# Sigmoid attention and a gated two-layer network on one core: the first group's keys loaded and transposed by slots, and one value product moved

## The chip, the cores and the metric

The kernel runs on one core of a Trainium2 chip. A core has five engines that work side by side, each through its own list of instructions in order: TensorE (PE in the profile; PEld is its weight load), VectorE (DVE), ScalarE (ACT), GpSimd (POOL) and SyncE (SP). Engines wait for one another through semaphores. Data moves between the chip's memory and the core's SBUF by 16 DMA engines; transfers are asked for by an instruction on SP (queue q1, "hardware dynamic" in the profile) or on POOL (queue q0, "software dynamic", which here also casts float32 to float16 on the way). Matmuls write PSUM. The metric is the device time of one execution in microseconds (us), the median of three.

## The reference: what is computed

```
scores = q @ k^T / sqrt(64) - log(448)        # 8 batches, 12 heads, 448 tokens, head size 64
attn   = sigmoid(scores)                      # no softmax: each entry by itself
x      = (attn @ v), heads side by side       # 3584 tokens x 768
h      = x @ w_in                             # 768 x 2048
g      = h * sigmoid(beta * h)
out    = g @ w_out                            # 2048 x 768, float32
```

## The kernel before

**Groups, slots, visits.** Four heads make a group (three groups a batch, 24 in all), two heads a slot. A group's q and k lie in SBUF as a tile `raw` of 128 rows: 32 rows for each head, and each row holds 14 tokens of that head side by side. So slot 0 of a group is rows 0 to 63, slot 1 rows 64 to 127. DVE transposes 32x32 blocks of pairs of float16 (`transpose`, L186 to L205) into `qT` and `kT`, where the tokens lie along the row and the head size along the partitions, in two halves e = 0, 1 that are added up in PSUM. The 448 keys of a head are cut in three tiles of 128 (jt = 0, 1, 2) and a rest of 64 (jt = 3, `JF`).

A visit computes scores for a group and lets ACT take the sigmoid. In the first batch the queries are taken in two halves of 224 (`QH`), and there a `half_visit` does two key tiles of both slots for one half: with second = 0 the tiles 0 and 1, with second = 1 tile 2 and the rest. Its matmuls (`score`, L213) each use 32 rows of the PE array, so four of them, two heads of two slots, stand beside one another. `weigh` (L224) is ACT's sigmoid over the score tile. The score tiles are PSUM buffers, three at first and two later. `attend` (L281) multiplies attention by the values of a group and has DVE cast the result to `xT` (L290).

**The dense layers** are cut into units: `dense1` (one 128-column chunk of the first layer with its sigmoid on ACT, L307, and product on DVE, L310) and `dense2` or `strassen` pieces of the second layer, all through L166. A list of these units in a fixed order, `fill`, is drawn on between the visits; `fill_units(n)` takes the next n.

**The start, written out by hand.** The stretch that the change touches is under `manual_schedule`: the program's order is each engine's order.

- SP loads the first half of group 0's queries and all of its keys as float32 into a staging place in the tile `gt` (L519), then the small beta vector (L548).
- POOL clears a small tile `dummy` (L525), with which ACT loads its sigmoid table (L526).
- PE runs `idle_units`: matmuls on a tile of zeros (`still`, L535), 9 ahead of the first visit and 4 or 2 behind each of the next ones.
- DVE casts the staged queries (L539) and transposes them; ACT and DVE cast half of the keys each (L541, L542); DVE transposes the keys in two instructions (L199, L203).
- POOL asks for everything else, one request behind the other: group 1's and 2's first query halves and keys (L110), the values (L131, L138), the second query halves, eight pieces of w_in (L148); later, behind waits for free buffers, the next group's q and k, two pieces of w_out (L156), the next values, and so on.
- Six half visits with the idle units between them, then the products with the values and the second query halves. From `share_psum(ctx, 2, 4)` on, half visits, dense units and `attend` calls alternate as the code lists them, up to the loop over all other visits, which a budget of estimated costs paces.

POOL's requests take turns on eight completion semaphores, so a request also waits until the one eight before it has landed.

Of the kernel before, what the change touches and what calls it, by code (L numbers as in the profile page):

```python
# [8 lines left out]
FP32 = mybir.dt.float32  # L9
FP16 = mybir.dt.float16  # L10
# [3 lines left out]
def kernel(  # L14
# [17 lines left out]
    P = 128  # L32
# [73 lines left out]
    def load_one(g: int, r: int, c0: int = 0, c1: int = NB):  # L106
        b, t = divmod(g, QPB)
        if g not in raws:
            raws[g] = rawp.tile([P, 2, NB, D], FP16, tag="raw", name="raw")
        nc.gpsimd.dma_start(  # L110
            out=raws[g][:, r, c0:c1].rearrange("p c d -> p (c d)"),
            in_=(q, k)[r][b, HQ * t : HQ * (t + 1)].rearrange("h (p c) d -> (h p) (c d)", c=NB)[
                :, c0 * D : c1 * D
            ],
        )
# [70 lines left out]
    def transpose(g: int, r: int, c0: int = 0, c1: int = NB):  # L186
        raw = raws[g][:, r]
        if r == 0:
            if g not in qT:
                qT[g] = qTp.tile([P, NB * BLK, PAIR], FP16, tag="qT", name="qT")  # L190
            nc.vector.transpose(  # L191
                out=in_order(g // QPB, qT[g][:, c0 * BLK : c1 * BLK]),
                in_=raw[:, c0:c1].rearrange("p c d -> p (c d)").bitcast(FP32),
            )
            return
        kT[g] = kTp.tile([P, S, PAIR], FP16, tag="kT", name="kT")
        to = kT[g].rearrange("p k e -> p (k e)").bitcast(FP32)
        frm = raw.rearrange("p c d -> p (c d)").bitcast(FP32).rearrange("p (c f) -> p c f", c=NB)
        nc.vector.transpose(  # L199
            out=to[:, 0 : JF * P].rearrange("p (j i q) -> p i j q", j=JF, i=HQ),  # L200
            in_=frm[:, 0:NF].rearrange("p (i j) f -> p i j f", j=JF),
        )
        nc.vector.transpose(  # L203
            out=to[:, JF * P :], in_=frm[:, NF:].rearrange("p c f -> p (c f)")
        )  # L205

    def score_tile():
# [41 lines left out]
                at_tiles[s, jt, 0] = at  # L249


    def half_visit(g: int, c0: int, second: int):
        slots = (2 * g, 2 * g + 1)
        scos = [score_tile() for _ in slots]
        plan = [(s, jt, sco, jt * QH) for jt in (0, 1) for s, sco in zip(slots, scos)]
        widths = [S, S]
        if second:
            plan = [(s, 2, sco, 0) for s, sco in zip(slots, scos)]
            plan += [(s, JF, scos[0], QH) for s in slots]
            widths = [S, QH]  # L260
        for i in range(0, len(plan), 2):
            for e in range(PAIR):
                for s, jt, sco, u0 in plan[i : i + 2]:
                    for hh in range(2):
                        score(sco, u0, s, jt, hh, e, c0, QH)
        ats = {id(sco): weigh(sco, n) for sco, n in zip(scos, widths)}
        for s, jt, sco, u0 in plan:
            at_tiles[s, jt, c0] = ats[id(sco)][:, :, u0 : u0 + QH]

    def attend(g: int, c0: int, n: int, part=(0, 1)):  # L270
        b, t = divmod(g, QPB)
        if b not in xTs:
            xTs[b] = xTp.tile([P, NHC, S], FP16, tag="xT", name="xT")
        slots = [2 * g + x for x in part]
        avs = [bank("av_ps") for _ in slots]
        todo = [(s, av, jt) for s, av in zip(slots, avs) for jt in range(JF)]
        for s, av, jt in todo + [(s, av, JF) for s, av in zip(slots, avs)]:
            at = at_tiles.pop((s, jt, c0))
            base, nk = (last_base(s), KL) if jt == JF else (0, P)
            for hh in range(2):  # L280
                nc.tensor.matmul(  # L281
                    av[hh * D : (hh + 1) * D, 0:n],
                    vs[b][base : base + nk, 2 * (s % NPAIR) + hh, jt],
                    at[base : base + nk, hh, 0:n],
                    start=(jt == 0),
                    stop=(jt == JF),
                    tile_position=(base, hh * D),
                )
        for s, av in zip(slots, avs):
            nc.vector.tensor_copy(out=xTs[b][:, s % NPAIR, c0 : c0 + n], in_=av[:, 0:n])  # L290
# [210 lines left out]
    def fill_units(n: int):  # L501
        for _ in range(n):
            fill[at_fill[0]][2]()
            at_fill[0] += 1
# [4 lines left out]
    with tc.manual_schedule():  # L509
        raws[0] = rawp.tile([P, 2, NB, D], FP16, tag="raw", name="raw")  # L510
        wide = gt.rearrange("p a b -> p (a b)").bitcast(FP32)
        cut = NH * D
        early = [(0, 0, NH), (1, 0, NB)]
        staged = {}
        at = 0
        for r, c0, c1 in early:
            staged[r] = wide[:, at : at + (c1 - c0) * D]
            at += (c1 - c0) * D
            nc.sync.dma_start(  # L519
                out=staged[r],  # L520
                in_=(q, k)[r][0, 0:HQ].rearrange("h (p c) d -> (h p) (c d)", c=NB)[
                    :, c0 * D : c1 * D
                ],
            )
        nc.gpsimd.memset(dummy, 0.0)  # L525
        nc.scalar.activation(out=dummy, in_=dummy, func=AF.Sigmoid, bias=0.0, scale=1.0)  # L526

        still = const.tile([P, 512], FP16, name="still")
# [4 lines left out]
        def idle_units(n: int):  # L533
            for _ in range(n):
                nc.tensor.matmul(idle, still[:, 0:P], still, start=True, stop=True)  # L535

        idle_units(9)
        raw = raws[0].rearrange("p r c d -> p r (c d)")
        nc.vector.tensor_copy(out=raw[:, 0, 0:cut], in_=staged[0])  # L539
        transpose(0, 0, 0, NH)  # L540
        nc.scalar.copy(out=raw[:, 1, cut:], in_=staged[1][:, cut:])  # L541
        nc.vector.tensor_copy(out=raw[:, 1, 0:cut], in_=staged[1][:, 0:cut])  # L542
        transpose(0, 1)
        for g in range(1, QPB):
            load_one(g, 0, 0, NH)
            load_one(g, 1)
        load_v(0)
        nc.sync.dma_start(out=beta_in[0:NDC], in_=moe_beta.rearrange("(c p) -> c p", p=P))  # L548
        for g in range(QPB - 1):
            load_one(g, 0, NH, NB)  # L550
        for c in range(WCH):
            if c == WCH // 2:
                load_one(QPB - 1, 0, NH, NB)
            load_w_in(c)
        for g in range(1, QPB):
            transpose(g, 0, 0, NH)
            transpose(g, 1)

        for g in range(QPB):
            for second in range(2):  # L560
                half_visit(g, 0, second)
                if 2 * g + second < 2 * QPB - 1:
                    idle_units(4 if g < QPB - 1 else 2)
        double_v_last(0)
        transpose(0, 0, NH, NB)
        attend(0, 0, QH)
# [20 lines left out]
        share_psum(ctx, 2, 4)  # L587
        fill_units(4)
        half_visit(1, QH, 0)
        fill_units(3)  # L590
        half_visit(1, QH, 1)
        transpose(2, 0, NH, NB)
        attend(0, QH, QH)
        fill_units(1)
        half_visit(2, QH, 0)
        fill_units(4)
        half_visit(2, QH, 1)
        attend(1, QH, QH)
        fill_units(3)
        attend(2, QH, QH)  # L600
        fill_units(1)
        transpose(QPB, 0)
# [97 lines left out]
```

## Time and profile before

| what | us |
|---|---|
| median of three runs | 383.44 (382.74 to 384.87) |
| the profiled execution | 383.27 |
| its span, first to last instruction | 381.5 |
| PE busy | 375.9 (99% of the span) |
| DVE, ACT, POOL busy | 231.9, 229.2, 66.4 |
| first real matmul (L213) starts at | 5.77 |
| first sigmoid (L224) starts at | 6.50 |

PE counts as busy in the idle units too. In the profile, a row of the timeline is: start, length, engine, line, operation, output <- inputs, shapes, how many instructions are merged in the row, and in brackets how long the engine was idle before it and what ended that. A row of a window is: the stretch, its length, then for PE, PEld, DVE, ACT and POOL the busy time with the number of instructions, then PE's granted clock (1.00 is full), the mean busy share of the DMA engines (packets that overlap count twice, so it can be over 1) and GB/s. A row of the chain of waits is: start, length, who held the chain that ended last.

### The profile page before, as it was taken

Reading aid. Unit: us, or ns where it says so; the run is one execution under the profiler, and the core shown is the slowest. Engines: PE = TensorE matmul, PEld = TensorE weight load, DVE = VectorE, ACT = ScalarE, POOL = GpSimd, SP = SyncE. Lnnn points to the kernel's source line nnn. Section 1 sums busy time; section 2 is a strip of 40 time slices with the busy share of each in tenths; the row PEclk is TensorE's granted clock in tenths of the full one; section 3 lists DMA queues with packets and bytes.
Section 4 is the critical chain, followed back from the end, with each engine's and each line's share of the span. In section 5 each row is a group of like instructions: output and inputs, shape, how many; then the busy total and the mean of one; then the engine's idle time right before and its main releaser. Section 6 shows DMA issues by size and latency. Waiting matters only on the chain.

```text
span 381.5 us, 8227 instructions
## 1 busy us (share of the span) xinstructions
PE 375.9 (99%) x3415; PEld 199.0 (52%) x3415; DVE 231.9 (61%) x439; ACT 229.2 (60%) x330; POOL 66.4 (17%) x114
## 2 busy tenths in 40 slices
PE   8999999999999999999999999999999999999996
PEld 3477744444654445444554445544455444555563
DVE  4357366775765557465775657665676665755761
ACT  5987756687356776577355792477752787435100
POOL 7842433140110410040110410112100000000000
PEclk9999999999999999999999999999999999999999
DMA  9999999755363930672363850649203300030033
GB/s 169 187 197 205 192 204 210 164 71 54 50 132 84 121 51 2 131 98 24 50 132 72 115 69 2 133 87 117 50 0 84 85 1 2 2 83 0 2 83 125
DMA packets 42405, 34.71 MB, mean 91 GB/s; under 512 B 21872, under 2 KB 38656, under 8 KB 42368
## 3 DMA queue, kind: packets, MB, share of 16 engines
q0 software_dynamic: 36688, 22.47, 43.5%
q1 hardware_dynamic: 5680, 11.71, 11.6%
q8 instruction: 27, 0.44, 0.5%
q14 instruction: 10, 0.08, 0.1%
HBM read 45.62 MB, written 11.01 MB: 148 GB/s over the span
## 4 chain that ended last, share of the span: by engine, by line
PE 88%; DMA 9%; POOL 1%; issue 0%; DVE 0%; POOLq 0%
PE m_ps L166 70%; PE sco L213 10%; PE av_ps L281 8%; DMA w_out<-in_moe_w_out_dram 5%; DMA w_in<-in_moe_w_in_dram 3%; DMA raw<-in_k_dram 2%; POOL w_in L148 1%; POOL raw L110 1%; POOL w_out L156 0%; DVE osb L342 0%; POOL dummy L525 0%; POOLq L684 0%
## 5 line engine op out<-in xcount | busy, mean ns | idle before, releaser
L224 ACT ACTIVATE attnT<-sco 128x896 f16<-128x896 f32 (+1 forms) x171 | 145.3, 902 | 81.2 <-PE sco L213 80.6
L166 PE MATMUL m_ps<-xT,w_in 128*128 128x448 f16 (+2 forms) x1014 | 154.7, 336 | 0.1
L310 DVE TENSOR_TENSOR gt<-m_ps,sg 128x448 f16<-128x448 f32 (+1 forms) x144 | 81.4, 572 | 81.1 <-ACT sg L307 77.6
L166 PEld LDWEIGHTS <-w_in 128*128 128x128 f16 (+1 forms) x1014 | 82.6, 101 | 68.8 <-issue 15.0
L307 ACT ACTIVATE sg<-m_ps,beta_sb 128x448 f32<-128x448 f32 (+1 forms) x144 | 84.2, 597 | 36.5 <-PE m_ps L166 29.5
L166 PEld LDWEIGHTS <-sum 128*64 128x64 f16 (+1 forms) x664 | 48.0, 104 | 33.6 <-issue 7.9
L213 PE MATMUL sco<-qT,kT 32*128 32x448 f16 (+3 forms) x864 | 51.9, 340 | 0.7 <-DVE kT L199 0.6
L166 PE MATMUL m_ps<-w_T,sum 128*128 128x384 f16 (+1 forms) x360 | 51.6, 327 | 0.0
L110 POOL DMA_DIRECT2D raw<-in_q_dram x26 | 14.3, 552 | 184.1 <-DVE kT L203 176.9
L430 DVE TENSOR_TENSOR osb<-m_ps,osb 128x384 f32<-128x384 f32 x60 | 33.3, 555 | 18.7 <-PE m_ps L166 16.9
L166 PEld LDWEIGHTS <-gt 128*128 128x128 f16 (+1 forms) x414 | 31.4, 103 | 24.0 <-issue 6.5
L281 PE MATMUL av_ps<-attnT,v 128*64 128x448 f16 (+3 forms) x432 | 40.2, 338 | 0.0
L400 DVE TENSOR_TENSOR sum<-gt 128x1024 f16<-128x1024 f16 x60 | 39.2, 678 | 0.1
L290 DVE CAST xT<-av_ps 128x448 f16<-128x448 f32 (+1 forms) x54 | 28.5, 568 | 15.2 <-PE av_ps L281 14.1
L166 PE MATMUL m_ps<-w_T,gt 128*64 128x384 f16 (+1 forms) x268 | 34.3, 327 | 0.0
L166 PE MATMUL m_ps<-w_out,sum 128*64 128x384 f16 (+1 forms) x304 | 33.8, 327 | 0.0
L281 PEld LDWEIGHTS <-v 128*64 128x64 f16 (+1 forms) x432 | 20.6, 108 | 18.8 <-issue 9.4
L213 PEld LDWEIGHTS <-kT 32*128 32x128 f16 (+1 forms) x864 | 13.7, 96 | 28.6 <-issue 26.0
L166 PE MATMUL m_ps<-w_out,gt 128*128 128x384 f16 (+3 forms) x146 | 22.7, 327 | 0.1
L131 POOL DMA_DIRECT2D v<-in_v_dram x32 | 19.8, 631 | 9.6 <-DMA w_in<-in_moe_w_in_dram 5.2
L191 DVE STREAM_TRANSPOSE qT<-raw 128x448 f32<-128x448 f32 (+1 forms) x27 | 16.7, 617 | 0.1
L433 ACT COPY osb<-m_ps 128x384 f32<-128x384 f32 x12 | 5.8, 481 | 16.8 <-DMA out_dram<-osb 8.6
(25 smaller groups left out, 90.0 us busy)
## 6 DMA issues: line engine op xcount, KB each, us to landing
out_dram<-osb SPq DMA_DIRECT2D x98, 96.0 KB, 1.9
raw<-in_k_dram POOLq DMA_DIRECT2D x23, 224.0 KB, 4.9
raw<-in_q_dram POOLq DMA_DIRECT2D x21, 224.0 KB, 3.8
v<-in_v_dram POOLq DMA_DIRECT2D x32, 144.0 KB, 6.7
w_in<-in_moe_w_in_dram POOLq DMA_DIRECT2D x8, 384.0 KB, 11.2
w_out<-in_moe_w_out_dram POOLq DMA_DIRECT2D x4, 768.0 KB, 13.0
v<-in_v_dram POOLq DMA_DIRECT2D x16, 48.0 KB, 6.4
out_dram<-osb SPq DMA_DIRECT2D x2, 384.0 KB, 3.0
```

The costliest lines, as they stand in the source:

```text
L110: nc.gpsimd.dma_start(out=raws[g][:, r, c0:c1].rearrange("p c d -> p (c d)"), in_=(q, k)[r][b, HQ * t : HQ * (t + 1)].rearrange("h (p c) d ...
L131: nc.gpsimd.dma_start(out=vs[b][i * BLK : (i + 1) * BLK, :, 0:JF].rearrange("p h j d -> p h (j d)"), in_=rows[:, :, JF * i * D : JF * (i + ...
L166: nc.tensor.matmul(to[c : c + step], hidden[:, c : c + step], weights, **({} if step == P else {"tile_position": (0, c)}), **flags,)
L191: nc.vector.transpose(out=in_order(g // QPB, qT[g][:, c0 * BLK : c1 * BLK]), in_=raw[:, c0:c1].rearrange("p c d -> p (c d)").bitcast(FP32),)
L213: nc.tensor.matmul(sco[base : base + nk, hh, u0 : u0 + n], kT[g][lo : lo + BLK, jt * P : jt * P + nk, e], qT[g][lo : lo + BLK, c0 : c0 + n ...
L224: nc.scalar.activation(out=at[:, :, 0:n], in_=sco[:, :, 0:n], func=AF.Sigmoid, bias=NEG_LOG_S, scale=MSCALE,)
L281: nc.tensor.matmul(av[hh * D : (hh + 1) * D, 0:n], vs[b][base : base + nk, 2 * (s % NPAIR) + hh, jt], at[base : base + nk, hh, 0:n], start ...
L290: nc.vector.tensor_copy(out=xTs[b][:, s % NPAIR, c0 : c0 + n], in_=av[:, 0:n])
L307: nc.scalar.activation(out=sg[:, 0:n], in_=m1[:, 0:n], func=AF.Sigmoid, bias=0.0, scale=beta_sb[:, dc : dc + 1])
L310: nc.vector.tensor_tensor(out=gt[:, dc, off : off + n], in0=m1[:, 0:n], in1=sg[:, 0:n], op=ALU.mult)
L400: nc.vector.tensor_tensor(out=sums[t, i], in0=x, in1=y, op=op)
L430: nc.vector.tensor_tensor(out=out, in0=in0, in1=in1, op=op)
```

## The change

- Group 0's keys come in two transfers, 64 rows (one slot) each, behind the queries' half. In the staging tile the keys now lie ahead of the queries.
- The clearing of `dummy` moves from POOL to DVE.
- The idle units ahead of the first visit are 8 in place of 9; one stands between the two slots of the first half visit, and 2 in place of 4 behind it.
- `transpose_keys` transposes key tiles j0 to j1 of some rows. For group 0: slot 0's tiles 0 and 1 are cast by ACT and transposed; then slot 1's (one tile cast by ACT, one by DVE) and transposed; then tile 2 and the rest of both slots are cast by DVE and transposed.
- The first half visit does all its matmuls of slot 0, then one idle unit, then those of slot 1, each with its own score tile; two matmuls stand side by side in place of four.
- Groups 1 and 2: keys are asked for ahead of the queries, and the transposes go tiles 0 to 2, queries, rest.
- The second query half of group 2 is asked for behind the fifth piece of w_in in place of the fourth.
- `attend(0, QH, QH)` goes right behind the next half visit, `half_visit(1, QH, 0)`; the fill units around it are dealt out anew (4, 3, 3, 3, 2, 1, 4 in place of 4, 3, 1, 4, 3, 1, 4) and stay 20 in all.

```diff
--- before.py
+++ after.py
@@ -193,15 +193,23 @@
                 in_=raw[:, c0:c1].rearrange("p c d -> p (c d)").bitcast(FP32),
             )
             return
-        kT[g] = kTp.tile([P, S, PAIR], FP16, tag="kT", name="kT")
-        to = kT[g].rearrange("p k e -> p (k e)").bitcast(FP32)
-        frm = raw.rearrange("p c d -> p (c d)").bitcast(FP32).rearrange("p (c f) -> p c f", c=NB)
+        transpose_keys(g, 0, JF, slice(0, P))
+        transpose_keys(g, JF, JF + 1, slice(0, P))
+
+    def transpose_keys(g: int, j0: int, j1: int, rows):
+        if g not in kT:
+            kT[g] = kTp.tile([P, S, PAIR], FP16, tag="kT", name="kT")
+        to = kT[g][rows].rearrange("p k e -> p (k e)").bitcast(FP32)
+        frm = raws[g][rows, 1].rearrange("p c d -> p (c d)").bitcast(FP32)
+        frm = frm.rearrange("p (c f) -> p c f", c=NB)
+        if j0 == JF:
+            nc.vector.transpose(
+                out=to[:, JF * P :], in_=frm[:, NF:].rearrange("p c f -> p (c f)")
+            )
+            return
         nc.vector.transpose(
-            out=to[:, 0 : JF * P].rearrange("p (j i q) -> p i j q", j=JF, i=HQ),
-            in_=frm[:, 0:NF].rearrange("p (i j) f -> p i j f", j=JF),
-        )
-        nc.vector.transpose(
-            out=to[:, JF * P :], in_=frm[:, NF:].rearrange("p c f -> p (c f)")
+            out=to[:, j0 * P : j1 * P].rearrange("p (j i q) -> p i j q", i=HQ, q=BLK),
+            in_=frm[:, 0:NF].rearrange("p (i j) f -> p i j f", j=JF)[:, :, j0:j1],
         )
 
     def score_tile():
@@ -249,7 +257,7 @@
                 at_tiles[s, jt, 0] = at
 
 
-    def half_visit(g: int, c0: int, second: int):
+    def half_visit(g: int, c0: int, second: int, between=None):
         slots = (2 * g, 2 * g + 1)
         scos = [score_tile() for _ in slots]
         plan = [(s, jt, sco, jt * QH) for jt in (0, 1) for s, sco in zip(slots, scos)]
@@ -258,9 +266,14 @@
             plan = [(s, 2, sco, 0) for s, sco in zip(slots, scos)]
             plan += [(s, JF, scos[0], QH) for s in slots]
             widths = [S, QH]
-        for i in range(0, len(plan), 2):
+        if between:
+            plan = [x for sco in scos for x in plan if x[2] is sco]
+        step = 1 if between else 2
+        for i in range(0, len(plan), step):
+            if i == 2 and between:
+                between()
             for e in range(PAIR):
-                for s, jt, sco, u0 in plan[i : i + 2]:
+                for s, jt, sco, u0 in plan[i : i + step]:
                     for hh in range(2):
                         score(sco, u0, s, jt, hh, e, c0, QH)
         ats = {id(sco): weigh(sco, n) for sco, n in zip(scos, widths)}
@@ -509,20 +522,23 @@
     with tc.manual_schedule():
         raws[0] = rawp.tile([P, 2, NB, D], FP16, tag="raw", name="raw")
         wide = gt.rearrange("p a b -> p (a b)").bitcast(FP32)
-        cut = NH * D
-        early = [(0, 0, NH), (1, 0, NB)]
-        staged = {}
-        at = 0
-        for r, c0, c1 in early:
-            staged[r] = wide[:, at : at + (c1 - c0) * D]
-            at += (c1 - c0) * D
+        k0 = wide[:, 0 : NB * D].rearrange("p (c d) -> p c d", c=NB)
+        q0 = wide[:, NB * D : (NB + NH) * D].rearrange("p (c d) -> p c d", c=NH)
+
+        def flat(t):
+            return t.rearrange("p c d -> p (c d)")
+
+        by_slot = [slice(x * P // 2, (x + 1) * P // 2) for x in range(2)]
+        nc.sync.dma_start(
+            out=flat(q0),
+            in_=q[0, 0:HQ].rearrange("h (p c) d -> (h p) (c d)", c=NB)[:, 0 : NH * D],
+        )
+        for x, rows in enumerate(by_slot):
             nc.sync.dma_start(
-                out=staged[r],
-                in_=(q, k)[r][0, 0:HQ].rearrange("h (p c) d -> (h p) (c d)", c=NB)[
-                    :, c0 * D : c1 * D
-                ],
-            )
-        nc.gpsimd.memset(dummy, 0.0)
+                out=flat(k0[rows]),
+                in_=k[0, 2 * x : 2 * x + 2].rearrange("h (p c) d -> (h p) (c d)", c=NB),
+            )
+        nc.vector.memset(dummy, 0.0)
         nc.scalar.activation(out=dummy, in_=dummy, func=AF.Sigmoid, bias=0.0, scale=1.0)
 
         still = const.tile([P, 512], FP16, name="still")
@@ -534,33 +550,49 @@
             for _ in range(n):
                 nc.tensor.matmul(idle, still[:, 0:P], still, start=True, stop=True)
 
-        idle_units(9)
-        raw = raws[0].rearrange("p r c d -> p r (c d)")
-        nc.vector.tensor_copy(out=raw[:, 0, 0:cut], in_=staged[0])
+        idle_units(8)
+        raw_q, raw_k = raws[0][:, 0], raws[0][:, 1]
+
+        def by_tile(t, rows, j0: int, j1: int):
+            return t[rows, 0:NF].rearrange("p (i j) d -> p i (j d)", j=JF)[:, :, j0 * D : j1 * D]
+
+        def cast_keys(copy, rows, j0: int, j1: int):
+            copy(out=by_tile(raw_k, rows, j0, j1), in_=by_tile(k0, rows, j0, j1))
+
+        nc.vector.tensor_copy(out=raw_q[:, 0:NH], in_=q0)
         transpose(0, 0, 0, NH)
-        nc.scalar.copy(out=raw[:, 1, cut:], in_=staged[1][:, cut:])
-        nc.vector.tensor_copy(out=raw[:, 1, 0:cut], in_=staged[1][:, 0:cut])
-        transpose(0, 1)
+        cast_keys(nc.scalar.copy, by_slot[0], 0, 2)
+        transpose_keys(0, 0, 2, by_slot[0])
+        cast_keys(nc.scalar.copy, by_slot[1], 0, 1)
+        cast_keys(nc.vector.tensor_copy, by_slot[1], 1, 2)
+        transpose_keys(0, 0, 2, by_slot[1])
+        every = slice(0, P)
+        cast_keys(nc.vector.tensor_copy, every, 2, JF)
+        nc.vector.tensor_copy(out=raw_k[:, NF:], in_=k0[:, NF:])
+        transpose_keys(0, 2, JF, every)
+        transpose_keys(0, JF, JF + 1, every)
         for g in range(1, QPB):
+            load_one(g, 1)
             load_one(g, 0, 0, NH)
-            load_one(g, 1)
         load_v(0)
         nc.sync.dma_start(out=beta_in[0:NDC], in_=moe_beta.rearrange("(c p) -> c p", p=P))
         for g in range(QPB - 1):
             load_one(g, 0, NH, NB)
         for c in range(WCH):
-            if c == WCH // 2:
+            if c == WCH // 2 + 1:
                 load_one(QPB - 1, 0, NH, NB)
             load_w_in(c)
         for g in range(1, QPB):
+            transpose_keys(g, 0, JF, every)
             transpose(g, 0, 0, NH)
-            transpose(g, 1)
+            transpose_keys(g, JF, JF + 1, every)
 
         for g in range(QPB):
             for second in range(2):
-                half_visit(g, 0, second)
+                first = 2 * g + second == 0
+                half_visit(g, 0, second, (lambda: idle_units(1)) if first else None)
                 if 2 * g + second < 2 * QPB - 1:
-                    idle_units(4 if g < QPB - 1 else 2)
+                    idle_units(2 if first else 4 if g < QPB - 1 else 2)
         double_v_last(0)
         transpose(0, 0, NH, NB)
         attend(0, 0, QH)
@@ -587,16 +619,16 @@
         share_psum(ctx, 2, 4)
         fill_units(4)
         half_visit(1, QH, 0)
+        attend(0, QH, QH)
         fill_units(3)
         half_visit(1, QH, 1)
         transpose(2, 0, NH, NB)
-        attend(0, QH, QH)
-        fill_units(1)
+        fill_units(3)
         half_visit(2, QH, 0)
-        fill_units(4)
-        half_visit(2, QH, 1)
         attend(1, QH, QH)
         fill_units(3)
+        half_visit(2, QH, 1)
+        fill_units(2)
         attend(2, QH, QH)
         fill_units(1)
         transpose(QPB, 0)
```

## The prediction

> **What bounds the kernel now.** I read the page first: PE is busy for 99% of the span, so what the kernel costs is PE's own work plus whatever holds PE up. The next view is the chain of waits over the first 60 us, because the change lies there:
>
> ```profile
> 1.26 1.71 POOL raw L110 x3
> 2.96 6.43 DMA raw<-in_k_dram
> ...
> 12.70 10.47 DMA w_in<-in_moe_w_in_dram
> ...
> 24.34 18.36 DMA w_out<-in_moe_w_out_dram
> 42.71 0.04 issue
> 42.75 1.46 PE m_ps L166 x8
> ```
>
> Each row is a start, a length and who held the chain. Up to 42.71 us the chain is not PE but the stream of POOL's loads, one request behind the other; from 42.75 us to the end it is PE. So the end is the landing of the second w_out request (42.71) plus 338.8 us of PE work and the last store. The timeline shows what PE does before that:
>
> ```profile
> 1.19 4.02 PE L535 MATMUL idle_ps<-still 128*128 128x512 f16 x9 [1.19 <-DVE still L529]
> 1.26 0.67 POOL L110 DMA_DIRECT2D raw<-in_q_dram  x1 [0.42 <-issue]
> ...
> 4.54 0.56 ACT L541 CAST raw<-gt 128x448 f16<-128x448 f32 x1 [2.31 <-DMA gt<-in_k_dram]
> ...
> 5.77 0.69 PE L213 MATMUL sco<-qT,kT 32*128 32x224 f16 x16 [0.56 <-DVE kT L199]
> ...
> 6.40 1.04 PE L535 MATMUL idle_ps<-still 128*128 128x512 f16 x4
> 6.50 9.49 ACT L224 ACTIVATE attnT<-sco 128x896 f16<-128x896 f32 x12 [1.40 <-PE sco L213]
> ```
>
> ACT runs twelve sigmoids back to back from 6.50 to 15.99, and PE's idle units at L535 fill the time between the visits. How much room PE has in front of the load stream is read from matmul groups of one kind:
>
> ```profile
> 26.66 2.70 PE L166 MATMUL m_ps<-xT,w_in 128*128 128x224 f16 x24
> ...
> 37.09 2.47 PE L166 MATMUL m_ps<-xT,w_in 128*128 128x224 f16 x24
> ...
> 41.17 3.04 PE L166 MATMUL m_ps<-w_out,gt 128*128 128x384 f16 x16
> ...
> 52.94 1.80 PE L166 MATMUL m_ps<-w_out,gt 128*128 128x384 f16 x10
> ```
>
> The 24 matmuls at 26.66 take 0.23 us more than the same 24 at 37.09: they wait inside for a w_in request (issued at 14.90, 13.1 us to landing, so 28.0). Ten matmuls of 128x384 take 1.80 us, a step each of 0.162 us, so sixteen should take 2.77; at 41.17 they take 3.04, a wait of 0.27 for w_out. Together PE is 0.50 us early for the load at 42.71. A PE that is earlier still only waits longer; one that is later by under 0.50 us costs nothing.
>
> Then the stream itself. Windows of the page's DMA columns, with share of the 16 engines and GB/s last in each row:
>
> ```profile
> 2.50:3.70 1.20, 1.20 (x4) 0.40 (x3) 0.29 (x1) 0.00 (x0) 1.20 (x3) 1.00 1.03 384
> 4.80:5.80 1.00, 0.44 (x5) 0.04 (x8) 0.85 (x3) 0.30 (x1) 1.00 (x2) 1.00 0.84 129
> 6.00:14.00 8.00, 7.82 (x105) 3.19 (x98) 2.38 (x8) 7.21 (x10) 6.11 (x9) 1.00 1.45 184
> 251.80:255.70 3.90, 3.90 (x27) 1.76 (x26) 2.14 (x5) 3.08 (x5) 0.08 (x1) 1.00 0.85 199
> 377.90:378.60 0.70, 0.14 (x2) 0.00 (x0) 0.42 (x1) 0.00 (x0) 0.00 (x0) 1.00 0.91 354
> ```
>
> SP's two 128-row loads for group 0 run at 384 GB/s. POOL's loads start weakly (129) and then run at 184 GB/s without a break. The last two rows are SP's stores: at 251.8 to 255.7 each takes 32 rows of SBUF, at 377.9 to 378.6 it takes 128. And by queue, from 2.5 to 3.7 us there is only one:
>
> ```profile
> q1 hardware_dynamic: 164, 0.46, 103.3%
> ```
>
> No packet of POOL's queue, although its first request was issued at 1.26.
>
> **The keys in two transfers.** Before: q's half, 224 KB, and all of k, 448 KB, each over 128 rows. After: k as two transfers of 224 KB over 64 rows each. SP spends one more issue of 0.42 us (the row of k's issue, 1.18 to 1.60); it ends at about 2.0 while q and the first slot keep the engines busy past 3; beta's request moves back by as much, lands at 6.4 in place of 5.9 and is wanted at 19.46. Both hidden. The rate over 64 rows is nowhere in this trace. From below: 384 GB/s as for 128 rows, no change. From above: the 32-row stores, 199 GB/s at a share of 0.85, so 234 at a full one, and a like window at 239.4 gives 202 at 0.91, so 222. At 222 the two slots take 2 x 229/222 = 2.06 us in place of 458/384 = 1.19, that is +0.87. I take +0.87, since SP's own 32-row transfers are nearest in queue and shape. That row has a weakness: SP issues a 96 KB store every 0.45 us, which alone limits them to 216 GB/s; but the engines' share at that rate speaks for slow packets. [...]
>
> **POOL one step earlier.** The memset of dummy leaves POOL (0.10 us at 0.73, and 0.42 of issue behind it) and goes to DVE, so POOL's first load goes out 0.10 to 0.52 us earlier. On DVE it puts the idle operand `still` back by about 0.1. In a quiet stretch a POOL load issued at 80.36 moves nothing before 81.50 and is moving after it, so the first one here could move at about 2.5; it moved only when SP's loads were through. So I count 0 for it, bounds -0.52 and 0. [...]
>
> **What the stream gets back.** Its first weak microsecond, 129 in place of 184 GB/s, is 55 KB, or 0.30 us. With SP's queue running at half rate that start lies beside it: -0.30, bounds -0.30 and 0. Sum for the stream: 0.87 + 0 - 0.30 = +0.57.
>
> **PE's front.** q is unchanged (3.38). Key bytes of slot 0 follow it: all of k landed at 4.51; half of it at 222 GB/s lands at about 4.51 - 1.19 + 1.03 = 4.35. ACT casts 512 columns (0.56 x 512/448 = 0.64), DVE transposes 256 of 384 columns (0.58 x 2/3 = 0.39, taken 0.45), so the first score comes at about 5.5 in place of 5.77. But a slot alone fills 64 rows of the array: its 8 matmuls go in four steps of two, and both slots need eight steps where there were four, 4 x 0.10 to 0.165 us = 0.4 to 0.66 more. Idle units fall from 9 + 4 to 8 + 1 + 2, two fewer, at 0.22 warm (1.04 for four, the last ending 0.38 after its start) or 0.42 cold (4.02 for nine, 0.63 for the last). That nearly cancels. Slot 1 lands at about 5.4; two casts (0.35) and 0.45 of transpose let it start at 6.25, and the third tile and the tail (two casts, two transposes, some 1.1 us of DVE) are ready at 7.35, where the second half visit starts now (7.37). So the third sigmoid stays near 8.2, within 0.2 us. PE's room of 0.50 covers that; it costs nothing.
>
> **Order behind the visits.** k goes before q in the loads of groups 1 and 2, 224 and 112 KB exchanged, and their first visits start at 9.07 and 12.28 against landings at 7.4 and 9.4: covered even by a stream 0.9 later (8.3 + 0.41 of transpose). The last query half of group 2 goes behind one more w_in request (0.53 us of stream), which brings that weight forward by as much and moves the query transpose to about 26.1, wanted at about 27.2. The values of group 0's second half, 16 matmuls of 0.92 us in all, move ahead of three dense units; the fill units are 20 before and after. By the steps of the rows (0.58 a unit, 0.51 to 0.63 a half visit) the last two w_in requests (15.71 + 14.3 = 30.0 and 17.43 + 14.5 = 31.9) are still met on landing, PE goes on at 32.0 as now, and 10.5 us of work lead to the w_out load again. Worth 0.
>
> **Sum.** 383.27 + 0.57 = 383.84 for the profiled execution; that one lies 0.17 below the median of the three runs (383.44), so 384.0 for a median. A measurement of this kernel can tell about 0.5%, 1.9 us, from no change.
>
> **Rivals.** *Full rate over 64 rows:* then the 0.87 falls away; the stream moves by 0 to -0.82 (both other terms), of which PE can follow at most 0.50 of room plus 0.15 of an earlier front. 382.8 to 383.4, about 383.1. For it: POOL's loads of v into 32 rows land 0.8 us apart for 144 KB, about as fast by the byte as its 128-row loads. Against it: the pair of store windows. *The change does not do what it says:* the first slot's scores start no earlier because its half transfer takes nearly as long as the whole did. That is part of my forecast. *Slower:* the second slot's keys get in line behind POOL's first request, which now goes out earlier and is the 224 KB of keys. Place: L213 of the first visit, second slot. POOL's first two requests needed from about 3.75 to 7.43 to land; a second slot that has to see most of this through lands as late as 7.9 in place of 5.4, ACT has no second score tile, and PE arrives at w_out 2.4 us late, less its room 0.50: 383.44 + 1.9 = 385.4 and up to 385.8. It decides from a landing of about 5.9 on (room used up) and is told from no change from 7.9 on. Against it: SP's queue went first throughout in this trace. *In between:* a landing at 6 to 7.5, 383.6 to 385.
>
> **How the numbers follow.** Forecast (stream later by 0.2 to 1.0) 0.52; full rate 0.28; in between 0.08; slower past 385.36 0.09; a gain past 1.9 us, for which no row offers a source, 0.03. Forecast and full rate reach from 382.8 to 384.5; one more unknown is the slowest of the 16 engines, whose lag makes the second w_out request land 4.7 us behind the first while a w_out request late in the stream needs about 3.9, so 0.4 us either way on top: 382.5 to 385.1. That leaves the slower rival and the large gain out. Faster by over 0.5% 0.03, within it 0.87, slower 0.10.
>
> **What would show it.** Right, if SP's key loads run near 200 GB/s, POOL's first packet comes later than 3.76 though its issue is earlier, the chain still goes through w_out, and its landing moves by about +0.6. Wrong, if the first slot's cast starts before 4.1 (full rate), if POOL's packets lie among SP's, if the chain before 40 us is PE and ACT, or if the idle units keep their 0.42 us step past 6.5 us.

## The result: slower, and the profile after

The changed kernel takes 387.49 us (median of six runs, 386.61 to 387.99) against 383.96 us for the kernel before, run beside it: a ratio of 1.0102, 95% interval 1.0080 to 1.0125. (The ratio is worked out from all runs of both kernels; the two medians alone would give 1.0092.) The forecast was 384.0 with a range of 382.5 to 385.1. The profiled execution took 386.61 us with a span of 384.8 us, against 383.27 and 381.5 before. It is the fastest of the six.

The chain of waits of the changed kernel, first 60 us (start, length, who held the chain):

```profile
1.18 4.88 DMA gt<-in_k_dram
6.08 0.63 ACT raw L560
6.73 0.45 DVE kT L210
...
7.23 0.92 PE sco L221 x6
8.15 0.54 PE idle_ps L551
...
11.52 1.50 PE idle_ps L551 x4
```

Before, this stretch belonged to POOL's load stream, up to the landing of w_out at 42.71. Now the first slot's keys hold it up to 6.06, and behind their cast and transpose it is almost only PE. The stream itself is not late: the same w_out request lands at 41.81, 0.90 us earlier than before. PE is what comes late to it. The timeline of the front and of the first w_out group (start, busy time, engine, line, operation, count, and in brackets the idle time before it and what ended that):

```profile
1.23 3.60 PE L551 MATMUL idle_ps<-still 128*128 128x512 f16 x8 [1.23 <-DVE still L545]
1.23 0.67 POOL L110 DMA_DIRECT2D raw<-in_k_dram  x1 [0.78 <-POOLq L716]
...
6.08 0.62 ACT L560 CAST raw<-gt 64x512 f16<-64x512 f32 x1 [3.85 <-DMA gt<-in_k_dram]
...
7.23 0.93 PE L221 MATMUL sco<-qT,kT 32*128 32x224 f16 x8 [2.40 <-DVE kT L210]
...
10.45 1.08 PE L221 MATMUL sco<-qT,kT 32*128 32x224 f16 x16
...
11.46 1.57 PE L551 MATMUL idle_ps<-still 128*128 128x512 f16 x4
...
44.81 2.76 PE L166 MATMUL m_ps<-w_out,gt 128*128 128x384 f16 x16
```

Three things are to be seen. The first score starts at 7.23 in place of 5.77, after 2.40 us in which PE had nothing to do. And PE is still at the half rate of its first idle units: eight score matmuls take 0.93 us, and the four idle units at 11.46 take 1.57 us, where the four at 6.40 took 1.04 before. And the sixteen w_out matmuls take 2.76 us, sixteen plain steps, so PE waits for no load there any more.

The loss can be followed along the half visits. First score +1.46 us (7.23 against 5.77); from there to the second half visit 3.22 us against 1.60, +1.62; to the third (12.96 against 9.07) 2.51 against 1.70, +0.81. That is 3.89 us. The 0.50 us of room in front of w_out covers part, and the ninth w_out matmul, which started at 42.75 before, starts at 46.11 (44.81 and eight steps of 0.162): +3.36 us. The span is 3.3 us longer.

Why the keys are late is in the packets. DMA queues of the changed kernel from 2.5 to 3.7 us (packets, MB, packet time as a share of 16 engines; q1 is SP's queue, q0 POOL's):

```profile
q0 software_dynamic: 35, 0.06, 54.5%
q1 hardware_dynamic: 79, 0.14, 40.8%
```

Before, q1 had this window to itself with 164 packets and 0.46 MB. Now POOL's first packet comes at 2.61 us where it came at 3.76, although POOL issued its first load at nearly the same time (1.23, and 1.26 before). The engines are nearly as busy as before (a share of 0.95 against 1.03), but they move 172 GB/s in place of 384, since POOL's packets hold them longer for a byte: 0.06 MB in 54.5% of 1.2 us is about 92 GB/s at a full share, SP's are at about 286, both estimates from these rows. Slot 0 lands at 6.06 and slot 1 at 7.33; the forecast had 4.35 and 5.4.

The bytes are not lost, they are others. From 2.6 to 6.0 us the kernel before (first row) and the changed one (second row) move the same in all, 232 and 234 GB/s:

```profile
2.60:6.00 3.40, 2.84 (x15) 0.81 (x16) 2.04 (x6) 0.56 (x1) 3.39 (x6) 1.00 1.04 232
...
2.60:6.00 3.40, 2.22 (x6) 0.49 (x4) 0.81 (x2) 0.00 (x0) 3.36 (x6) 1.00 1.06 234
```

Before, the keys went first and POOL's loads after them; now the two go together, and the keys are through only at the end.

### The profile page after: what moved, and what is told of

Same layout as the page of the kernel before. It is cut to its first block, busy times and chain, and to the rows that moved or that the text cites. A ratio compares the mean times of both kernels' runs of the same rounds, so it can differ in the third digit from the quotient of the medians.

```text
span 384.8 us, 8231 instructions
## 1 busy us (share of the span) xinstructions
PE 377.5 (98%) x3413; PEld 199.6 (52%) x3413; DVE 232.5 (60%) x444; ACT 229.9 (60%) x331; POOL 66.3 (17%) x113
## 4 chain that ended last, share of the span: by engine, by line
PE 96%; DMA 1%; ACT 1%; DVE 0%; issue 0%; SPq 0%; ACTq 0%
PE m_ps L166 74%; PE sco L221 12%; PE av_ps L294 9%; PE idle_ps L551 1%; DMA gt<-in_k_dram 1%; ACT attnT L232 0%; ACT raw L560 0%; DVE kT L210 0%; DVE osb L355 0%; DVE gt L323 0%; SPq L532 0%; ACT sg L320 0%; ACTq L320 0%
## 5 line engine op out<-in xcount | busy, mean ns | idle before, releaser
L221 PE MATMUL sco<-qT,kT 32*128 32x448 f16 (+3 forms) x864 | 53.3, 344 | 2.6 <-DVE kT L210 2.4
## 6 DMA issues: line engine op xcount, KB each, us to landing
w_in<-in_moe_w_in_dram POOLq DMA_DIRECT2D x8, 384.0 KB, 10.6
out_dram<-osb SPq DMA_DIRECT2D x2, 384.0 KB, 3.3
```

What stands on the lines that cost most here:

```text
L221: nc.tensor.matmul(sco[base : base + nk, hh, u0 : u0 + n], kT[g][lo : lo + BLK, jt * P : jt * P + nk, e], qT[g][lo : lo + BLK, c0 : c0 + n ...
```

## The experiments

Two losses were to be told apart, late keys and a slow PE, and for the late keys several causes: 64 rows in a transfer (the prediction's estimate of 222 GB/s against the 384 measured over 128 rows), POOL's packets among SP's, and what lets them in. Of that last there were two versions: that group 0's loads now take a third request of hardware queues, whatever its shape (F below), and that the request which goes out behind POOL's first one is the one that suffers (G). The kernel before was run again beside each group of experiments; its medians were 383.22 (beside the first four), 383.00 (the next four), 383.54 (slot 1 on ACT's queue, the keys as third request, 11 units alone) and 383.37 (POOL held with 11 units, and the last one).

### Only the two key transfers, in the kernel before

```diff
...
-                out=staged[r],
...
+            for x in range(1 + r):
+                rows = slice(x * P // 2, (x + 1) * P // 2) if r else slice(0, P)
+                nc.sync.dma_start(
+                    out=staged[r][rows],
...
```

> The kernel before, with one edit: group 0's keys come in two transfers of 64 rows. Theory A (transfers over 64 rows are slow and share the DMA engines with POOL's loads): the slots land at about 6.0 and 7.3 us as in the changed kernel; all casts here wait for both, so the first score comes at 8 us or later in place of 5.8 and PE sits idle for over 2 us; 2 to 4 us slower, 386 to 388. Rival B (what let POOL's loads in early was their new order or their earlier issue, not the row count): POOL's first packet stays at 3.7, the slots land by 5.5, the first score by 6.8, 383.5 to 384.5. Rival C (the order by slots of casts and matmuls costs the time, not the transfers): as before, 383 to 384.2.

Measured: 387.52 us, ratio 1.0106 [1.0076, 1.0135]: the whole loss of the change. POOL's first load is issued at 1.26, as in the kernel before, yet its first packet comes at 3.19 and lies among SP's. The slots land at 5.67 and 7.97. All work of the first visit needs both, so the first score comes at 9.29 after 4.46 us of idle PE. The casts, transposes and scores by slot, the memset and the order behind the visits are thus not needed for the loss.

### The change with the keys in one transfer

```diff
-        for x, rows in enumerate(by_slot):
-            nc.sync.dma_start(
...
+        nc.sync.dma_start(
+            out=flat(k0), in_=k[0, 0:HQ].rearrange("h (p c) d -> (h p) (c d)", c=NB)
+        )
```

> The changed kernel, with group 0's keys in one transfer of 128 rows and all else as changed. Theory A: keys land at 4.4 to 4.7 us, POOL's first packet at about 3.7 again, first score by 6, time within 0.5 us of the kernel before, 383 to 384.5. Rival B: POOL's first packet stays at 2.6 and mixes with the keys, which land after 5.5; 385 to 387. Rival C: keys land by 4.7 and the kernel is still 2 us or more slower, 386 to 387.5.

Measured: 384.41 us, ratio 1.0025 [1.0003, 1.0047]. The keys land at 4.54 and the first score starts at 5.71. DMA queues of this kernel from 2.5 to 3.7 us:

```profile
q1 hardware_dynamic: 177, 0.48, 105.7%
```

SP's queue is alone again, with POOL's load issued at 1.23 as in the changed kernel. So the memset, which takes POOL's first issue from 1.26 to 1.23 only, lets nobody in. What is left of the loss goes with the clock: in its profiled execution (386.00 us) four idle units at 9.95 still take 1.89 us, and with 11 idle units nothing of it can be seen any more (below).

### The change with 18 idle units at the start

```diff
-        idle_units(8)
+        idle_units(18)
```

> The changed kernel with 18 idle units ahead of the first visit in place of 8, so that PE is busy until slot 0's keys come. If the half clock after the gap is a cause of its own (theory A's second half): idle units step at 0.43 us up to about 6 us and at 0.22 from there, they end at about 7.3, all later idle units step at 0.22, and the front loses only the late keys: 1.5 us less the room of 0.5 at the w_out load, so about 1 us slower than before, 384.5 to 385.5. If the clock is no cause, ten more units only add to the front or change nothing: 387 to 388.5.

Measured: 385.12 us, ratio 1.0039 [1.0018, 1.0059]. The keys are about as late as in the changed kernel (5.88 and 7.71), the first score starts at 7.05, but its eight matmuls take 0.57 us and four idle units 1.04. So of the loss of 1.02% the half rate is about 0.63%, some 2.4 us, and the late keys 0.39%, some 1.5 us; both ratios carry an interval of about 0.2% either way, and with them this split. Between the two profiled executions the difference is smaller, 1.6 us in the span (384.8 and 383.2): that of the changed kernel was its fastest run, 0.88 us below its median.

### Only the order behind the visits, in the kernel before

```diff
-            if c == WCH // 2:
+            if c == WCH // 2 + 1:
...
         half_visit(1, QH, 0)
+        attend(0, QH, QH)
         fill_units(3)
...
-        attend(0, QH, QH)
-        fill_units(1)
+        fill_units(3)
         half_visit(2, QH, 0)
-        fill_units(4)
-        half_visit(2, QH, 1)
         attend(1, QH, QH)
         fill_units(3)
+        half_visit(2, QH, 1)
+        fill_units(2)
```

> The kernel before, with only the second part of the change: the value product of group 0's second half behind the next half visit, the fill units dealt out anew, the last query half one piece of w_in later. Theory A and B: within 0.3 us of before, PE still held by the w_out load at 42.7. Rival C (this part costs): over 0.7 us slower, with PE waits on sigmoids between 22 and 37 us.

Measured: 383.08 us, ratio 0.9992 [0.9974, 1.0010]. This part is worth nothing, as forecast.

### The change with POOL held back

Two memsets of an unused buffer ahead of POOL's first load, 1.39 us each.

```diff
+        for _ in range(2):
+            nc.gpsimd.memset(ws["T7"].rearrange("p a b -> p (a b)").bitcast(FP32), 0.0)
         nc.vector.memset(dummy, 0.0)
```

> The changed kernel with two memsets of an unused tile on POOL ahead of its first load, so that POOL's loads go out 2 to 3 us later. Only the landings of the keys are asked for. Theory A (two causes: a 64-row transfer runs at some 200 GB/s even alone, and POOL's loads take turns with it): alone, slot 0 lands at 4.3 to 4.7 and slot 1 at 5.3 to 5.8, in place of 6.1 and 7.3. Rival D (no sharing matters; 64 rows are simply that slow): they land at 6 and 7.3 as before this edit. Rival E (64 rows are not slow at all, sharing is everything): slot 0 by 4.1, slot 1 by 4.7.

Measured in a single execution: POOL's first load at 3.49, its first packet at 4.86. The slots land at 4.69 and 5.59, in place of 6.06 and 7.33. The timeline of this kernel:

```profile
4.71 0.62 ACT L562 CAST raw<-gt 64x512 f16<-64x512 f32 x1 [2.48 <-DMA gt<-in_k_dram]
...
5.61 0.40 ACT L562 CAST raw<-gt 64x256 f16<-64x256 f32 x1 [0.28 <-DMA gt<-in_k_dram]
...
5.85 0.57 PE L221 MATMUL sco<-qT,kT 32*128 32x224 f16 x8 [1.03 <-DVE kT L210]
```

Both casts follow their slot at once and the first score starts at 5.85. So most of the lateness is POOL's packets (7.33 less 5.59, 1.74 us for the second slot), and the smaller part is the two transfers themselves: without POOL the second slot lands 1.08 us behind the one transfer of before (5.59 against 4.51). The first slot, which the change wanted early, lands at 4.69 even so, 0.18 us behind the whole of the keys before. The kernel's own time, 385.12 us, is no gain, since the held stream now ends it: w_out lands at 44.61.

### Two key transfers by columns, 128 rows each

```diff
-        early = [(0, 0, NH), (1, 0, NB)]
+        early = [(0, 0, NH), (1, 0, NH), (1, NH, NB)]
...
```

> The kernel before, with group 0's keys in two transfers by columns: 128 rows each, 7 of the 14 tokens of a row, so the same 224 KB a transfer as a slot. Theory A: full rate over 128 rows, both landed by 4.8, POOL's first packet at about 3.7, time within 0.5 us of before. Rival F (it is the second transfer as such, one more issue on SP, that lets POOL's loads in between): the second lands after 5.5, first score after 6.8, 1 to 4 us slower.

Measured: 387.37 us, ratio 1.0096 [1.0068, 1.0124]. The first part lands at 3.87, ahead of all; the second, issued at 1.64, only at 7.39, with POOL's first packet at 3.15. First score 8.64. The loss needs no 64-row transfer; F held. So did G: the late request went out behind POOL's first one (1.64 and 1.26).

### The kernel before with a gap

```diff
-        idle_units(9)
+        idle_units(4)
```

> The kernel before, with 4 idle units ahead of the first visit in place of 9: the keys land as before and PE idles from about 3 us to 5.8. If a gap of about 2.5 us alone keeps the clock at half: idle units step at 0.43 us until 9 us or later, and the kernel loses 1 to 2.5 us with the same transfers, 384.5 to 386. If the gap is harmless: 383 to 383.6, units behind the first visit at 0.22.

Measured: 384.85 us, ratio 1.0033 [1.0008, 1.0057]. The timeline of this kernel:

```profile
1.19 1.89 PE L535 MATMUL idle_ps<-still 128*128 128x512 f16 x4 [1.19 <-DVE still L529]
...
5.74 0.93 PE L213 MATMUL sco<-qT,kT 32*128 32x224 f16 x16 [2.66 <-DVE kT L199]
6.60 1.89 PE L535 MATMUL idle_ps<-still 128*128 128x512 f16 x4
...
9.43 1.09 PE L535 MATMUL idle_ps<-still 128*128 128x512 f16 x4
```

The keys are on time (4.46) and the first score starts at 5.74, 0.03 earlier than before. But after 2.66 us without work PE stays at half rate to about 9.4, and that alone, its room of 0.50 already used, costs 1.85 us of the median, or 1.3 us by the ratio (0.3 to 2.2).

### The change with one transfer and 11 idle units

```diff
...
+        nc.sync.dma_start(
+            out=flat(k0), in_=k[0, 0:HQ].rearrange("h (p c) d -> (h p) (c d)", c=NB)
+        )
...
-        idle_units(8)
+        idle_units(11)
```

> The changed kernel with one transfer of 128 rows for group 0's keys and 11 idle units in place of 8, so that PE is busy until the keys come. Order by slots of casts, transposes and matmuls stays. Theory A: both causes gone, so within 0.4 us of before, 382.8 to 383.7. Rival C (order by slots costs by itself): still 0.8 us or more slower.

Measured: 383.54 us, ratio 1.0000 [0.9977, 1.0022]. With keys on time and PE warm, everything else in the change (casts, transposes and scores by slot, the order of loads and of the values) costs and gains nothing beyond the 0.2% of the interval.

### Slot 1 asked for by ACT's queue

```diff
-            nc.sync.dma_start(
+            (nc.sync, nc.scalar)[x].dma_start(
                 out=flat(k0[rows]),
```

> The changed kernel, with slot 1's keys asked for by ACT at its start in place of SP as its third request; row counts, order of work and idle units as changed. Theory G (a request on SP that goes out after POOL's first, at 1.2 to 1.9 us, moves its bytes by turns with POOL's slow casting loads, whatever its shape; that is what made the second transfer late): slot 1 goes out by 1.2 us, ahead of POOL, and both slots land by 4.5 to 5.7, POOL's first packet comes after 3.5; 383 to 385, at most 1.5 us over before, the rest being the clock. Rival A (64 rows are what makes it slow): slots stay past 6 us and the time past 386.

Measured: 388.85 us, ratio 1.0122 [1.0091, 1.0153]. ACT's slot 1 lands at 4.60; SP's slot 0, issued at 1.18 and so ahead of POOL's, lands at 7.40. First score 8.57. A miss: G fell as it was put, because the late request went out before POOL's, if only by 0.05 us (1.18 and 1.23; both issues are still running at 1.7). That there are three requests fits still.

### The same with 11 idle units

```diff
-        idle_units(8)
+        idle_units(11)
```

> The same as the kernel with slot 1 on ACT's queue, and 11 idle units in place of 8, so that PE is busy until slot 0's keys come. Theory G with the clock as second cause: both gone, within 0.5 us of before. If the by-slot work has a cost of its own after all: 0.8 us or more over before.

Measured: 388.20 us, ratio 1.0103 [1.0072, 1.0134]. Slot 0 lands at 7.00, the first score starts at 8.16 after 2.57 us of idle PE, and the half rate is back in spite of the units: PE's granted clock is 0.50 from 9 to 15 us, and four idle units at 12.27 take 1.89 us. A miss as well.

### The keys in one transfer, but as the third request

The kernel before with q's half in two pieces, so that k's one transfer over 128 rows is SP's third request.

```diff
-        early = [(0, 0, NH), (1, 0, NB)]
+        early = [(0, 0, 4), (0, 4, NH), (1, 0, NB)]
...
```

> The kernel before, with the queries' half of group 0 asked for in two pieces by columns, so that the keys, still one transfer of 448 KB over 128 rows, are SP's third request and go out at about 1.6 us in place of 1.2. Theory G: the same bytes in the same rows now share with POOL's loads; keys land at 6 to 8.5 us in place of 4.5, first score after 7.3, 2.5 to 5 us slower. Rival A (rows) or rival F (a second transfer of keys): keys land by 5.1 and the time stays within 0.6 us of before.

Measured: 386.96 us, ratio 1.0072 [1.0046, 1.0097]. The keys' transfer is untouched, yet it lands at 6.65. DMA queues of this kernel from 2.5 to 3.7 us:

```profile
q0 software_dynamic: 50, 0.04, 70.0%
q1 hardware_dynamic: 115, 0.09, 25.6%
```

POOL is in from 2.64 us and takes 70% of the engines' time. Neither the split of the keys nor their rows are needed: it suffices that the keys stand third. F in the form in which it was first expected, a second transfer of keys, falls here; what is left of it is the place in line.

### The change with POOL held for one memset, and 11 idle units

```diff
+        nc.gpsimd.memset(ws["T7"].rearrange("p a b -> p (a b)").bitcast(FP32), 0.0)
         nc.vector.memset(dummy, 0.0)
...
-        idle_units(8)
+        idle_units(11)
```

> The changed kernel, both transfers kept, with one memset of 1.4 us on POOL ahead of its first load and 11 idle units in place of 8. If late keys and the half clock are the whole loss: slots land by 5.2 and 6.2 us, idle units step at 0.22 from 7 us on, POOL's stream is about as late as before's, and the time is 0 to 1 us over before. If something else in the change costs: still 1.5 us or more over before with both gone.

Measured: 383.94 us, ratio 1.0003 [0.9987, 1.0019]. Both key transfers are kept. POOL's first load goes out at 2.05, its first packet at 4.20, and the slots land at 4.55 and 5.43. With the keys on time and PE at full rate (four idle units at 8.84 take 1.04 us) the loss is gone to within 0.2%: these two are the whole of it that can be seen. Against the kernel before with 11 units as well (next experiment, 0.9984) some 0.2% may be left, at the edge of both intervals. The first slot gains nothing by its landing at 4.55: the keys of before landed at 4.51, and the first score stands behind the idle units until 6.03.

### The kernel before with 11 idle units, and with the order behind the visits on top

```diff
-        idle_units(9)
+        idle_units(11)
```

> The kernel before with 11 idle units ahead of the first visit in place of 9, which closes PE's gap of 0.56 us before the first score. If some of before's runs (those near 384.5) lose their time to a clock that is slow to rise, that group of runs goes and the median is 0.2 to 0.6 us below before's; if that spread comes from the loads, no change within 0.2 us. The two more units cost at most 0.3 us at the first score, inside PE's room before the w_out load.

> The kernel before with 11 idle units and the second part of the change (value product moved, fill units dealt out anew, query half one piece of w_in later). If that part is worth nothing because the w_out load ends the stretch: the same as 11 idle units alone, 0 to 0.6 us below before. If it gains: 0.7 us or more below before.

Measured: 383.13 us, ratio 0.9984 [0.9970, 0.9998], for the units alone; 383.18 us, ratio 0.9986 [0.9972, 1.0001], with the order behind the visits (the edit of the fourth experiment). The first is the one version whose interval lies below 1, ahead by 0.16%. The first visit's sixteen score matmuls take 0.57 us in it in place of 0.69, and its runs end at 383.72, while six of the 18 of the kernel before beside it lie at 384.4 to 385.3. That fits a full rate that comes more surely with more work ahead of the visit; in the six slower runs themselves no trace shows it. The order behind the visits adds nothing here either.

## Why the prediction was wrong, step by step

**What bounds the kernel.** Right for before: the stream to 42.71, and PE 0.50 us ahead of it. The room is what the runs bear out: a late PE paid 3.36 us for 3.89, and the kernel with both slots on time (POOL held for one memset) paid nothing that can be seen.

**The keys in two transfers.** +0.87 us was a fair size (1.08 measured where POOL is held back by two memsets, 0.92 by one) and the wrong question. The term priced the transfer as if SP's queue stayed alone; it did not, and slot 1 landed at 7.33 in place of 5.4. And the loss came the same with 128-row transfers (a ratio of 1.0096, against 1.0106 with 64 rows).

**POOL one step earlier.** The first step that failed. "So I count 0 for it" was right of the memset: POOL's load went out 0.03 us earlier, and with one transfer SP still had the window to itself. What failed is the reason, "it moved only when SP's loads were through", taken as a rule that would hold for whatever SP queues. A row of the trace of before spoke against it and was read over. DMA issues of the kernel before in the first 9 us (last column: us from issue to landing):

```profile
gt<-in_k_dram SPq DMA_DIRECT2D x1, 448.0 KB, 3.3
...
beta_in<-in_moe_beta_dram SPq DMA_DIRECT2D x1, 8.0 KB, 4.3
```

SP's third request, 8 KB, needed longer than the 448 KB of keys ahead of it: issued at 1.64, landed at 5.94, after POOL's loads had begun at 3.76. I costed its landing "at 6.4 in place of 5.9" and did not ask why it was 5.9. The change puts the second slot in that third place (and beta fourth, where it landed at 7.69). In all seven kernels here that have a third load ahead of beta and do not hold POOL back, packets of POOL's lie among those of the hardware queues from 2.5 to 3.7 us: 35 beside 79 of SP's in the changed one, 4 to 50 in the seven. With two loads there are none: q1 is alone until 3.73 to 3.83.

**What the stream gets back.** Predicted later by 0.57 in sum, it is earlier by 0.90 at the w_out landing. POOL's packets began 1.15 us earlier (2.61 in place of 3.76), and what SP's keys lost by sharing, the stream had at first. That this is the whole reason is not shown: with the two transfers alone POOL's packets began 0.57 us earlier, and w_out landed 0.20 us later (42.91). The bound went from the stream to PE.

**PE's front.** The second step that failed, "it costs nothing". Slot 0 was to land at 4.35 and landed at 6.06, so the first score came at 7.23 in place of about 5.5. The step also took the idle units at 0.22 or 0.42 us alike and did not ask what a later score does to the rate: that is about 2.4 of the 3.9 us of the ratio.

**Order behind the visits.** Worth 0, and 0.9992 [0.9974, 1.0010] was measured.

**The rivals.** The slower one, at 0.09, had the place and the mechanism: slot 1's keys in line with POOL's first request, a landing of up to 7.9 (7.33 came, 7.97 with the transfers alone). It had two things wrong. It put the cause in POOL's earlier request, which was earlier by 0.03 us only; the place of the keys in SP's line was enough. And its price, 1.9 us, had no clock in it. Of the four signs named as showing the forecast wrong three came (POOL's packets among SP's, a chain mostly of PE before 40 us, idle units at a 0.42 step past 6.5 us); the fourth, a first cast before 4.1 us, did not: it came at 6.08.

**What stays open.** With two loads of hardware queues and POOL's first load at about 1.25 us, POOL's first packet came at 3.73 to 3.83 in all seven traces; with three it came at 2.61 to 3.33 in all seven. Why is not settled. The number of requests by itself is not the reason. The kernel before has a third one too, beta's, which was late itself and let nobody in. And with POOL held for one memset three loads, all issued ahead of POOL's at 2.05, were followed by POOL's first packet only at 4.20. Another reading fits more of the traces: the first two requests, or those that are handed to the engines ahead of POOL's, go first, and what comes behind them shares. When POOL's first packet came, hardware queues had started 0.62 to 0.66 MB of the first two loads' 0.69 in the seven traces with two; in those with three, 0.37 to 0.40 of 0.46 in five and 0.20 of 0.23 in the one with the keys third. The changed kernel's own trace, with 0.16 of 0.46, does not fit. The order in which the engines are handed the requests is in no trace.

## What to carry to other kernels

A queue that has the DMA engines to itself in the trace has them only for the requests that were there: before a transfer is cut in two, look where the request that would now stand next in line landed, however small it was (here beta's 8 KB, 4.3 us from issue to landing). The shared load was also a hole in TensorE's work, so the late first operand was charged twice here, some 1.5 us for the wait and some 2.4 us for the half rate behind it; count idle units to the latest landing and not to the usual one (11 of them ended at 5.59 us where slot 0 landed at 7.00, and the half rate came back). And where a profile shows another engine early by some room, say how far that engine may slip before it is the bound, and look at what would make it slip that far.

## What the runs showed of the hardware

TensorE's half rate stands in the granted clock of the rows only in part. In the kernel before and the changed one every row reads 1.00 up to 20 us, also where idle units of 512 columns take 0.43 us each and later 0.22; there the rate is read from the step of like matmuls. Where the clock had risen and fell again, the rows show it. Windows of the kernel with only the two key transfers, in which PE had no work from 4.83 to 9.29 us:

```profile
7.00:8.00 1.00, 0.00 (x0) 0.00 (x0) 0.00 (x0) 0.00 (x0) 0.00 (x0) 0.87 0.99 168
8.00:14.00 6.00, 4.71 (x39) 1.62 (x40) 2.86 (x10) 3.18 (x5) 4.58 (x7) 0.50 1.48 174
14.00:16.00 2.00, 2.00 (x23) 0.63 (x20) 1.02 (x2) 1.13 (x3) 2.00 (x4) 0.86 1.35 173
```

If the clock only went between 1.00 and 0.50 here, the means of 0.87 and 0.86 put the fall at 7.74 and the rise at 14.56, 6.8 us at half rate; that is an estimate from these rows. The mean clock of a run shows it too: with slot 1 on ACT's queue and 11 units, three runs with a mean of 0.991 took 388.07 to 388.50 us and the one with 0.996 took 386.19.

How long a gap has to be is not settled. A gap of 0.56 us ahead of the first score let the full rate come inside the first visit (sixteen score matmuls in 0.69 us, the four idle units behind them in 1.04); gaps of 2.40 and 2.66 us put it off to the units at 11.46 and to 9.4 us. One of 0.89 us put it off in one execution (one transfer, eight units: 1.89 us for four units at 9.95), while one of 1.03 us did not in another (POOL held, also eight units). In the first of these two PE then worked without a gap from 5.71 us, and the full rate came only within the units at 12.63. So gaps of about 1 us had both outcomes; what decides between them no row shows.

The mixed loads were the other surprise. From 2.5 to 3.7 us SP's loads alone moved 384 GB/s at a share of 1.03 of the engines; with POOL's first packets among them, at nearly the same share (0.95), 172 GB/s. That holds for the start of the mixture: from 3.8 to 6.0 us the changed kernel moved 269 GB/s, and the kernel before, with SP's loads nearly through, 153.
